# A gated recurrence and a gated linear unit: a deeper ring of squares, one x tile less, and batches of two chunks

## The chip, the core and the metric

The kernel runs on one core of a Trainium2 chip. Its engines work side by side, each through its own queue of instructions in order: TensorE (PE), VectorE (DVE), ScalarE (ACT) and GpSimd (POOL) compute, SyncE (SP) issues most of the transfers. The metric is the device time of one execution in microseconds (us); less is better.

## What is computed

The inputs are three arrays of 4 sequences, 6336 tokens and 256 features, and some small weights. In the reference's terms, cut to the core:

```python
a_t = np.exp(8.0 * sig_r * np.log(sigmoid(a_param)))      # decay, sig_r = sigmoid(r_gate)
norm = np.sqrt(np.maximum(1.0 - a_t * a_t, 1e-06))
x_gated = norm * sig_i * x                                # sig_i = sigmoid(i_gate)
h = a_t[:, t] * h + x_gated[:, t]                         # for every t: the recurrence, y[:, t] = h
gate = sigmoid(conv(y, conv_w))                           # causal, 5 taps
out = (gate * (y @ w_val)) @ w_out
```

## The kernel before

The 25344 tokens are cut into 51 tiles: 48 of 512 tokens, 3 of 256. A chunk is what one scan runs over: 23 chunks of two tiles (1024 tokens), and smaller ones at both ends (256, 512 at the front; 512, 256, 256 at the back; CHUNKS, L17). There are 28 chunks. The 256 features lie in two halves of 128 partitions, so most steps on a chunk come twice (index k = 2c + h).

A tile g or a chunk c passes through these steps, each a small function with a letter:

- load (l) and loadx (x) on SP: the gates r and i of a tile, and its x. NIN = 4 tiles of gates and NX = 5 tiles of x have buffers. store (s), also on SP, writes a tile of the output.
- tanh (t, ACT, L354): tanh of both gates at once, from which the sigmoids follow.
- u2 (u, L365 on DVE or L369 and L370 on POOL): (tanh + 1) times x, into a ring of NU = 10 tiles. The string U2 (L35) says for each tile which engine does it.
- srT (r, PE, L379): transposes of r's tanh; exp (e on ACT, L388): the decay a, into the ring aring.
- e (e on POOL, L396): a times a, into the ring ering, of NE × 512 = 4096 tokens.
- sq (q, ACT, L400): square roots, which make squares into norms in the same ring, in half the bytes. Tanh and exp lie in one table of ACT, the square root in another; ACT's table is loaded anew at each change between them. So the roots are done for several chunks at a time: UNITS (L19) says how many chunks each batch takes, and a batch is one activation, or two where its chunks are not in one piece of the ring (Shape, L92 to L103).
- nT (n, PE, L410): transposes of norms; xg (x, DVE, L417): norms times u; xT (x, PE, L426): transposes back.
- scan (s, DVE, L444): the recurrence, 1024 steps in one instruction, into yring.
- conv (c, PE, L470), tg (g, ACT, L478; tanh of the gate), val (v, PE, L486), gv (v, DVE, L496), out (o, PE, L508), and osb (o; DVE L519 or ACT L521), which copies a bank of output to SBUF for the store. The string OSB (L33) says for each of the 99 pieces of the output which engine copies it.

The order on each queue is written out by hand: ORDER (L48) holds one string of letters per engine, in which the n-th letter of a kind is the n-th job of that kind on that engine. BANK_ORDER (L61) says which of four PSUM banks each transpose or output uses. make_jobs (L130) lists the jobs with what each depends on: a tile's x load, for instance, on the input gate of tile g − NX, which frees its buffer; a square on the root and the transposes that last used its place in the ring (eold, L104). make_plan (L181) walks the strings with the costs of COST (L37) and gives all jobs in one order of start; the loop at L532 issues them. Only the strings decide the order on a queue. A queue waits where a job's inputs or its place are not there yet.

The setup ahead of the loop issues the first eight jobs of SP, makes the identity and the diagonal weights, and loads the weights wv (L292, four transfers) and wo (L296, two transfers) from POOL's queue, before POOL's first square.

Of the kernel before, what the change touches and what calls it, by code (L numbers as in the profile page):

```python
# [9 lines left out]
P = 128  # L10
# [5 lines left out]

CHUNKS = [[256], [512]] + [[512, 512]] * 23 + [[512], [256], [256]]  # L17

UNITS = [2, 1, 2, 3, 3, 3, 3, 3, 2, 2, 1, 3]  # L19
NS = 10  # L20
NE = 8
NU = 10
NY = 6
NIN = 4
NX = 5
NTR = 3
NTI = 5
NOSB = 3
# [1 line left out]
BANKS = 4  # L30
PB = dict(srT=2, nT=2, xT=2, ops=2)

OSB = "DDDDDDDDDDDAADDDDDDDDDDDDDDDDDDDDDDDDDDDDDDDDDDDDDDDDDDDDDADDDDDDDDDDAAAAADDDAAAADAAAAAADADDAAAADAA"  # L33

U2 = "DDPDDDPPDPPPPDPPPPPPPPPPPPPPDPPPPPPPPPPPPPPPPPPPPPP"  # L35

COST = dict(load=(0.05, 2.72), loadx=(0.02, 1.37), tanh=(0.11, 1.7), u2P=(0.2, 3.25), u2D=(0.2, 1.7), srT=(0.05,  # L37
            0.47), exp=(0.26, 0.86), e=(0.06, 1.83), sq=(0.2, 1.71), nT=(0.05, 0.5), xg=(0.02,
            0.58), xT=(0.05, 0.48), scan=(0.13, 2.14), conv=(0.22, 1.14), tg=(0.1, 0.83), val=(0.02,
            0.96), gv=(0.07, 1.07), out=(0.02, 0.49), osbD=(0.6, 0), osbA=(0.5, 0), store=(0.03,  # L40
            1.36))


LETTERS = dict(
    DMA=dict(l="load", x="loadx", s="store"), ACT=dict(t="tanh", e="exp", q="sq", g="tg", o="osb"),
    PE=dict(r="srT", n="nT", x="xT", c="conv", v="val", o="out"), POOL=dict(e="e", u="u2"),
    DVE=dict(u="u2", x="xg", s="scan", v="gv", o="osb"))
ORDER = dict(  # L48
    DMA=("llllxllxxxllxlxlxxxlxllxxsllxlsxxsslxlxslllsxxllssxxslslxlxxslslxsslxlxslxsllxslxsxsxlxsllxslxlslssx"
         "xlsxslxllssxsxxsllxlslsxxsxxsslsxlxslsssxxsssssssssss"),  # L50
    ACT=("teetetteeetqqttgeteetegtqegtetgetetgeettgqgetteogoetgtegtgeegtgqettegetgteegetgqgttgeetgtgetegeettgq"
         "getgettgeetgeetgtgqetgetgeettgeogqgtgetgetegtqogeoeogootgqgtteegoeogeeoeogqogoogoooggogooogogoo"),
    PE=("rrrrrrnxxnxcnxrrnrvxrcxovorcnnxorcvxnrrvncxoorrvooxcvocorovonnnnxrcxvonoxrconrvxcovxcrorxcvocvoocoov"
        "rooonnnxrxnrxnvcrnxvorcorovcxvoocxoooovnncnrnxxrcoxvorcvroxocrvrnoconvoxxocvroovnncnonrxxvcroxrncvoo"
        "rrnoxcoxvcoovcooxvronnvonorncoxrrvxcxvoorcoxonvcovnonoxcrvocxorvorncnnxxcooxrvonnvrocoxnoovxcovncovn"
        "oxrrcxvorocorrxcornvoxocvxonnvocxoovoxcnvocxooxvocoxvocoxovocvoo"),
    POOL="eeeeeeueeeeuuueueeeeeuuuuueeeeueeuuueeueeeeuuuuueueeeeeuuuueeueueeeuuueeueeuuueeueeuueeuuueeeueeeuu",
    DVE=("uuxssxsxuusxsvsvououxxsvoxsxvoosvoosovouooxxxvxssxvsxovsosvsvoooovoovooxxxosxssvxxsovoovsoovooosxoxv"
         "xxssvsoovosuxovooxvosvoosoxxvxoxssovsxoovxsoovsoovosovoxxoxoxvosvssovosvxooxoxovsovsvoxoxxsosovxxsvs"
         "vxsvoxoxovssvsxvosvxxvsvsxsovsosovsvsvov"))  # L60
BANK_ORDER = ("2220300232032030101322321213031230312121301103230301320123103021230121321321012121032312030131032110"  # L61
              "3203210321303123021032021023120103120130231030231023013203121032031230131302102302031031220131201321"
              "03120202310233203213201203302132002310232320202312303203031210")
TABLE, SEM, DMA_LAT = 1.3, 0.15, 2.2
START, ACT_START = 0.9, 4.6
FP32 = mybir.dt.float32
BF16 = mybir.dt.bfloat16
ACT = mybir.ActivationFunctionType
ALU = mybir.AluOpType


class Shape:
# [3 lines left out]
    def __init__(self, total, seq):  # L76
# [10 lines left out]
        self.apos, self.aold = self.place(NS * WIN)  # L87
        self.epos, _ = self.place(NE * WIN)
        self.ypos, self.yold = self.place(NY * WIN)


        self.runs, self.npos, batch_of = [], [], []  # L92
        for u, n in enumerate(UNITS):
            runs = []
# [35 lines left out]
def make_jobs(sh):  # L130
# [4 lines left out]
    jobs = {op: [] for ops in LETTERS.values() for op in ops.values()}  # L135
    unit_of = [u for u, n in enumerate(UNITS) for _ in range(n)]
    ends = [sum(UNITS[:u + 1]) for u in range(len(UNITS))]
    qlast = [max(q for q, (w, _) in enumerate(sh.pieces) if w == g) for g in range(len(sh.tiles))]
# [5 lines left out]
    for g, (_, n) in enumerate(sh.tiles):  # L144
        f = n / WIN
        c = sh.chunk_of[g]
        job("load", "DMA", f, [("tanh", g - NIN)])
        job("loadx", "DMA", f, [("u2", g - NX)])
        job("tanh", "ACT", f, [("load", g), ("u2", g - NTI)]
            + ([("srT", 2 * sh.chunk_of[g - NTR] + 1)] if g >= NTR else []))  # L150
        job("u2", "DVE" if U2[g] == "D" else "POOL", f, [("tanh", g), ("loadx", g)] + ([("xT", 2 * sh.chunk_of[g - NU] + 1)] if g >= NU else []), "u2" + U2[g])
        job("nT", "PE", f, [("sq", unit_of[c]), ("xg", g - PB["nT"])], None, 1)
        job("xg", "DVE", f, [("nT", g), ("u2", g)])
        job("conv", "PE", f, [("scan", 2 * c + 1), ("tg", g - 1)])
        job("tg", "ACT", f, [("conv", g), ("gv", g - 2)])
        job("val", "PE", f, [("scan", 2 * c + 1), ("gv", g - 1), ("conv", g)])
        job("gv", "DVE", f, [("tg", g), ("val", g)] + ([("out", qlast[g - 2])] if g >= 2 else []))
        job("store", "DMA", f, [("osb", q) for q, (w, _) in enumerate(sh.pieces) if w == g])
    for c, (_, n, g0, g1) in enumerate(sh.chunks):
# [3 lines left out]
        for h in range(2):  # L163
            k = 2 * c + h
            job("srT", "PE", f, [("tanh", g1 - 1), ("exp", k - PB["srT"])], None, 1)
            aold = ("scan", 2 * sh.aold[c] + h if sh.aold[c] >= 0 else -1)
            job("exp", "ACT", f, [("srT", k), aold])
            job("e", "POOL", f, [("exp", k), ("sq", eu), ("nT", sh.chunks[ed][3] - 1 if ed >= 0 else -1)])
            job("xT", "PE", f, [("xg", g1 - 1), ("scan", k - PB["xT"])], None, 1)
            job("scan", "DVE", f, [("xT", k), ("val", ylast - 1), ("conv", ylast)])  # L170
    for q, (g, i) in enumerate(sh.pieces):
        job("out", "PE", 1, [("gv", g), ("osb", q - PB["ops"])], None, 1)
        job("osb", "DVE" if OSB[q] == "D" else "ACT", 1, [("out", q), ("store", g - NOSB)], "osb" + OSB[q])
    for u, n in enumerate(UNITS):
        size = sum(sh.chunks[c][1] for c in range(ends[u] - n, ends[u])) / CHUNK
# [5 lines left out]
def make_plan(sh):  # L181
# [5 lines left out]
    for eng, letters in ORDER.items():  # L187
        todo = {op: [i for i, job in enumerate(jobs[op]) if job[0] == eng] for op in LETTERS[eng].values()}
        seq[eng] = [(op, todo[op].pop(0)) for op in (LETTERS[eng][x] for x in letters)]
        assert not any(todo.values())  # L190
    free_bank = iter(BANK_ORDER)
    for op, i in seq["PE"]:
# [5 lines left out]
    done, order, mode = {}, [], "E"  # L198
    free = dict(dict.fromkeys(seq, 0.0), DMA=START, ACT=ACT_START)
    at, left = dict.fromkeys(seq, 0), sum(len(ops) for ops in seq.values())  # L200
    while left:
        was = left
        for eng, ops in seq.items():
            while at[eng] < len(ops):
# [9 lines left out]
                free[eng] = t + dur  # L214
                done[op, i] = t + dur + (DMA_LAT if eng == "DMA" else 0.0)
                order.append((t, op, i, eng, dur))
# [8 lines left out]
def kernel(  # L225
# [11 lines left out]
    nc = tc.nc  # L237
    B, S, D = x.shape
    assert D == 2 * P, f"kernel assumes D == 256, got {D}"
    H = D // P  # L240
# [24 lines left out]
    def loadx(g):  # L265
        t0, nt = tiles[g]
        nj = nt // P
        xt = inp.tile([P, SUB, D], FP32, name="xt", tag="xt", bufs=NX)
        nc.sync.dma_start(xt[:, 0:nj, :], xf[t0:t0 + nt, :].rearrange("(p j) d -> p j d", j=nj))
        live["xt", g] = xt  # L270

    with tc.manual_schedule():
# [13 lines left out]
        b025 = const.tile([P, 1], FP32, name="b025")  # L286
        nc.vector.memset(b025[:], 0.25)
        wv = const.tile([P, H, D], BF16, name="wv")

        for hk in range(H):  # L290
            for m in range(H):
                nc.gpsimd.dma_start(wv[:, hk, m * P:(m + 1) * P].rearrange("p (h c) -> p h c", h=H),  # L292
                                    moe_w_val[hk * P:(hk + 1) * P, :].rearrange("p (h m c) -> p m h c", h=H, m=2)[:, m])
        wo = const.tile([P, H, D], BF16, name="wo")
        for h in range(H):
            nc.gpsimd.dma_start(wo[64 * h:64 * h + 64, :, :],  # L296
                                moe_w_out[h * P:(h + 1) * P, :].rearrange("(m c) n -> c m n", m=2))
        khf = const.tile([P, H], FP32, name="khf")
        wcol = const.tile([P, H, CONV_K], FP32, name="wcol")
        with tc.tile_pool(name="ps_setup", bufs=1, space=bass.MemoryType.PSUM) as ps_setup:  # L300
# [33 lines left out]

        ering = rings.tile([P, NE * WIN * H], FP32, name="ering")
        nring = ering[:].bitcast(BF16)
# [186 lines left out]
        def op_store(g, eng):  # L523
# [2 lines left out]
            nc.sync.dma_start(of[t0:t0 + nt, :].rearrange("(p j) d -> p j d", j=nj),  # L526
                              live.pop(("osb", g))[:, 0:nj, :])

        ops_by_name = dict(load=op_load, loadx=op_loadx, tanh=op_tanh, u2=op_u2, srT=op_srT, exp=op_exp, e=op_e, sq=op_sq,
                           nT=op_nT, xg=op_xg, xT=op_xT, scan=op_scan, conv=op_conv, tg=op_tg, val=op_val, gv=op_gv,  # L530
                           out=op_out, osb=op_osb, store=op_store)
        for (t, op, i, eng, dur) in plan:  # L532
            ops_by_name[op](i, eng)


# [28 lines left out]
```

## Time and profile before

| | |
|---|---|
| median of 6 runs | 315.68 us (313.38 to 317.97) |
| the profiled execution, its time | 315.39 us |
| its span, first to last instruction | 313.6 us |
| granted TensorE clock, mean | 0.964 |
| busy share: ACT, DVE, PE, POOL | 91%, 86%, 80%, 78% |
| DMA | 104.51 MB, mean 333 GB/s |

The profile is of one execution. A row of a group names the line, the engine, the operation, what it writes and reads with shapes, and how often; behind the bar come busy us and the mean duration in ns, then the idle time of the engine just before these instructions and what ended it. A wait for several things is put down to the one that came last. A busy PE is not PE at its peak, as matmuls are pipelined and their ends are modelled. The mean shares hide stages: the pipeline fills for some 45 us, runs, and drains over the last 30.

In the order of ACT's queue there are 24 table loads, 15 activations of roots in 11 groups, 51 tanhs of inputs, 56 exponentials, 51 tanhs of gates and 25 output copies.

### The profile page before, as it was taken

To read this page: it belongs to the slowest core of one execution; us is meant where nothing else is said; L and a number is where in the kernel's file an instruction comes from. 1 tells how busy PE (TensorE), PEld (TensorE's weight loads), DVE (VectorE), ACT (ScalarE), POOL (GpSimd) and SP (SyncE) were. 2 spreads that over 40 slices of the span, in tenths; PEclk is the share of its full clock that TensorE was granted. 3 is DMA by queue.
4 is the path that set the end of the run, shared out by engine and by line. 5 is a ranking of instruction groups with operands and counts; after the bars stand their busy time and mean duration, and the time that the engine had idled before them with its cause. 6 is when DMAs were issued, how large, how long until landed. Compare 5 with 4: busy or idle time off the path is not lost.

```text
span 313.6 us, 6572 instructions
## 1 busy us (share of the span) xinstructions
PE 249.9 (80%) x2561; PEld 163.2 (52%) x2591; DVE 269.5 (86%) x273; ACT 284.7 (91%) x224; POOL 245.1 (78%) x154
## 2 busy tenths in 40 slices
PE   1226765887699987996897889979899989999994
PEld 0113633554565655554654565647555755666562
DVE  4016899698999989999799899999999999998983
ACT  5799899599999999999999979999999999989553
POOL 6273599949998997899999989998997988986000
PEclk9999987799999998899899899999999999999998
DMA  7999997995999799999994999999979989843355
GB/s 234 356 397 412 409 408 293 398 344 184 366 416 414 301 301 418 420 367 375 420 413 171 324 418 414 380 382 376 416 261 366 415 298 314 324 141 144 136 203 202
DMA packets 30797, 104.51 MB, mean 333 GB/s; under 512 B 4391, under 2 KB 4654, under 8 KB 30766
## 3 DMA queue, kind: packets, MB, share of 16 engines
q1 hardware_dynamic: 29376, 103.82, 86.9%
q0 software_dynamic: 1376, 0.26, 1.0%
q8 instruction: 20, 0.33, 0.4%
q14 instruction: 11, 0.09, 0.1%
q10 hardware_dynamic: 14, 0.01, 0.0%
HBM read 78.39 MB, written 25.95 MB: 333 GB/s over the span
## 4 chain that ended last, share of the span: by engine, by line
ACT 32%; PE 23%; DVE 15%; issue 13%; POOL 9%; DMA 5%; SPq 1%; ACTq 0%; DVEq 0%; POOLq 0%
ACT tring L354 13%; PE gp L470 7%; ACT aring L388 6%; ACT ering L400 5%; POOL uring L370 5%; ACT tg L478 4%; DVE yring L444 4%; PE bank L508 4%; PE bank L410 4%; DVE osb L519 4%; POOL ering L396 3%; PE val L486 3%; DMA ri<-in_i_gate_dram 3%; DVE gv L496 3%; PE bank L426 3%
## 5 line engine op out<-in xcount | busy, mean ns | idle before, releaser
L396 POOL TENSOR_TENSOR ering<-aring 128x1024 f32<-128x1024 f32 (+2 forms) x56 | 95.5, 1721 | 35.4 <-ACT aring L388 35.4
L444 DVE TENSOR_TENSOR_SCAN yring<-aring,yring,bank 128x1024 bf16<-128x1024 f32 (+5 forms) x54 | 110.3, 2053 | 3.8 <-PE bank L426 3.7
L370 POOL TENSOR_TENSOR uring<-t,xt 128x1024 bf16<-128x1024 f32 (+1 forms) x43 | 100.8, 2345 | 4.4 <-DMA xt<-in_x_dram 0.9
L354 ACT ACTIVATE tring<-ri 128x2048 bf16<-128x2048 f32 (+1 forms) x51 | 94.3, 1865 | 1.0 <-DMA ri<-in_i_gate_dram 0.7
L470 PE MATMUL gp<-yring,diag 64*64 64x512 bf16 (+15 forms) x1196 | 68.5, 358 | 5.1 <-ACT tg L478 4.7
L388 ACT ACTIVATE aring<-bank,khf 128x1024 f32<-128x1024 bf16 (+2 forms) x56 | 61.0, 1115 | 9.7 <-PE bank L379 9.1
L508 PE MATMUL bank<-wo,gv 128*128 128x256 bf16 x396 | 58.4, 277 | 11.2 <-DVE osb L519 4.1
L496 DVE SCALAR_TENSOR_TENSOR gv<-tg,val 128x1024 bf16<-128x1024 bf16 (+1 forms) x54 | 60.5, 1124 | 6.2 <-PE val L486 4.2
L478 ACT ACTIVATE tg<-gp 128x1024 bf16<-128x1024 f32 (+1 forms) x51 | 51.3, 1005 | 8.9 <-PE gp L470 8.2
L508 PEld LDWEIGHTS <-gv 128*128 128x128 bf16 x396 | 37.2, 99 | 31.1 <-issue 16.9
L519 DVE TENSOR_SCALAR osb<-bank 128x512 f32<-128x512 f32 x74 | 48.8, 680 | 2.5 <-PE bank L508 2.1
L486 PE MATMUL val<-yring,wv 128*128 128x512 bf16 (+1 forms) x174 | 48.3, 381 | 2.9 <-DVE gv L496 0.8
L379 PE MATMUL bank<-ident_b,tring 128*128 128x128 bf16 x396 | 34.9, 235 | 17.9 <-ACT tring L354 9.0
L470 PEld LDWEIGHTS <-diag 64*64 64x64 bf16 x1196 | 31.2, 110 | 30.7 <-issue 16.0
L369 POOL TENSOR_SCALAR t<-tring 128x1024 f32<-128x1024 bf16 (+1 forms) x43 | 45.1, 1049 | 2.0
L400 ACT ACTIVATE ering<-ering,b 128x2048 bf16<-128x2048 f32 (+3 forms) x15 | 46.2, 3108 | 0.1
L410 PE MATMUL bank<-ident_f,ering 128*128 128x128 f32 x198 | 35.0, 308 | 12.5 <-ACT ering L400 8.0
L379 PEld LDWEIGHTS <-tring 128*128 128x128 bf16 x396 | 28.4, 105 | 26.5 <-ACT tring L354 13.7
L417 DVE TENSOR_TENSOR uring<-bank,uring 128x1024 bf16<-128x1024 bf16 (+1 forms) x51 | 33.3, 666 | 7.1 <-PE bank L410 7.0
L426 PE MATMUL bank<-ident_f,uring 128*128 128x128 f32 x198 | 33.3, 290 | 6.4 <-DVE uring L417 4.6
L410 PEld LDWEIGHTS bank<-ident_f,ering 128*128 128x128 f32 x198 | 28.1, 207 | 19.6 <-ACT ering L400 10.4
L365 DVE SCALAR_TENSOR_TENSOR uring<-tring,xt 128x512 bf16<-128x512 bf16 x15 | 19.8, 1362 | 15.6 <-DMA xt<-in_x_dram 15.6
(32 smaller groups left out, 104.5 us busy)
## 6 DMA issues: line engine op xcount, KB each, us to landing
ri<-in_r_gate_dram SPq DMA_DIRECT2D x48, 512.0 KB, 8.5
ri<-in_i_gate_dram SPq DMA_DIRECT2D x48, 512.0 KB, 9.1
xt<-in_x_dram SPq DMA_DIRECT2D x48, 512.0 KB, 9.0
out_dram<-osb SPq DMA_DIRECT2D x48, 512.0 KB, 5.0
ri<-in_r_gate_dram SPq DMA_DIRECT2D x3, 256.0 KB, 5.4
ri<-in_i_gate_dram SPq DMA_DIRECT2D x3, 256.0 KB, 5.3
xt<-in_x_dram SPq DMA_DIRECT2D x3, 256.0 KB, 4.2
out_dram<-osb SPq DMA_DIRECT2D x3, 256.0 KB, 2.7
```

The source lines that it names most:

```text
L354: nc.scalar.activation(out=tring[:, r:i + 1:i - r, 0:nj, :], in_=ri[:, :, 0:nj, :], func=ACT.Tanh, scale=0.5)
L370: nc.gpsimd.tensor_tensor(out=u.rearrange("p w d e -> p w e d"), in0=t1.rearrange("p (w e) d -> p w e d", e=2), in1=xt.rearrange("p (w e) ...
L379: nc.tensor.transpose(out=srT[:, col:col + P], in_=tring[:, g % NTR, j, h * P:(h + 1) * P], identity=ident_b[:])
L388: nc.scalar.activation(out=aring[:, h, a0:a0 + nt].rearrange("c (w p j) -> c w p j", p=P, j=nj), in_=live.pop(("srT", k))[:, 0:nt].rearran ...
L396: nc.gpsimd.tensor_tensor(out=ering[:, H * e0 + h * nt:H * e0 + (h + 1) * nt], in0=a, in1=a, op=ALU.mult)
L400: nc.scalar.activation(out=nring[:, 2 * H * e0:2 * H * e0 + H * m], in_=ering[:, H * e0:H * (e0 + m)], func=ACT.Sqrt, scale=-0.25, bias=b0 ...
L410: nc.tensor.transpose(out=nT[:, w * D + h * P:w * D + (h + 1) * P], in_=ering[:, n0 + w:n0 + nw * P:nw], identity=ident_f[:])
L444: nc.vector.tensor_tensor_scan(out=yring[:, h, y0 + c0:y0 + c1], data0=aring[:, h, a0 + c0:a0 + c1], data1=xT[:, c0:c1], initial=0.0 if fr ...
L470: nc.tensor.matmul(out=gp[64 * h:64 * h + 64, m, c0:c1], lhsT=diag[rows, h, kk, rows], rhs=yring[rows, h, src:src + c1 - c0], start=(sh == 0),
L478: nc.scalar.activation(out=tg[:, :, 0:nt], in_=live.pop(("gp", g))[:, :, 0:nt], func=ACT.Tanh, scale=0.5)
L496: nc.vector.scalar_tensor_tensor(out=gv[:, 0:nj, hs, :].rearrange("c j h p -> c j (h p)"), in0=tg[:, hs, 0:nt].rearrange("c h (p j) -> c j ...
L508: nc.tensor.matmul(out=ops[:, e * D:(e + 1) * D], lhsT=gv[:, 2 * i + e, hk, :], rhs=wo[:, hk, :], start=(hk == 0), stop=(hk == H - 1))
```

## The change

- NE goes from 8 to 10: the ring of squares and norms holds 5120 tokens. NX goes from 5 to 4: a tile of x in flight less.
- UNITS: 14 batches of two chunks each, where there were 12 batches of one to three.
- OSB, U2, ORDER and BANK_ORDER are new strings. OSB has 19 letters "A" (ACT) in place of 25; U2 still has eight "D" (DVE), at tiles 0 to 3, 5, 7, 8 and 20 in place of 0, 1, 3, 4, 5, 8, 13 and 28. COST has other figures for nT, xT, conv, val and out; they change only the order in which the program is built, not that on a queue.
- The weights wv and wo are loaded from POOL's queue after the second square (of chunk 0), in place of ahead of the first.

In the new order of ACT's queue there are 30 table loads and 16 activations of roots in 14 groups. The first eight jobs of SP are l l l x l l l x; they were l l l l x l l x.

```diff
-UNITS = [2, 1, 2, 3, 3, 3, 3, 3, 2, 2, 1, 3]
+UNITS = [2, 2, 2, 2, 2, 2, 2, 2, 2, 2, 2, 2, 2, 2]
-NE = 8
+NE = 10
-NX = 5
+NX = 4
-OSB = "DDDDDDDDDDDAADDDDDDDDDDDDDDDDDDDDDDDDDDDDDDDDDDDDDDDDDDDDDADDDDDDDDDDAAAAADDDAAAADAAAAAADADDAAAADAA"
+OSB = "DDDDDDDDDDDDDDDDDDDDDDDDDDDDDDDDDDDDDDDDDDDDDDDDDDDDDADDDDDDDDDDDDDDDDDDDDAAAAADDDDDAAAAAAAAAAADADA"
-U2 = "DDPDDDPPDPPPPDPPPPPPPPPPPPPPDPPPPPPPPPPPPPPPPPPPPPP"
+U2 = "DDDDPDPDDPPPPPPPPPPPDPPPPPPPPPPPPPPPPPPPPPPPPPPPPPP"
...
-    ACT=("teetetteeetqqttgeteetegtqegtetgetetgeettgqgetteogoetgtegtgeegtgqettegetgteegetgqgttgeetgtgetegeettgq"
-         "getgettgeetgeetgtgqetgetgeettgeogqgtgetgetegtqogeoeogootgqgtteegoeogeeoeogqogoogoooggogooogogoo"),
+    ACT=("teeteetqtteteetetgqteegtteettgqgetegetetgqgteegttgetegtgeqgteetgetgqgetettgeegtgqeegttgtegetgtegqegt"
+         "tgeetgtegqegttegetgoetgqegttegetgqgetegtgetgetgqeogetgootgoeoteegeqgeogeoqogogoogogooooggoo"),
...
-    POOL="eeeeeeueeeeuuueueeeeeuuuuueeeeueeuuueeueeeeuuuuueueeeeeuuuueeueueeeuuueeueeuuueeueeuueeuuueeeueeeuu",
+    POOL="eeeeeeeeueueeeuuueeeeuuuueeeueuuueeeeuueeeeuuuueeuueeuueueueeueueueueeuueueeuuueeueeuuueueeeeuueeeuu",
...
+WEIGHTS_AFTER = ("e", 1)
...
-        for hk in range(H):
-            for m in range(H):
-                nc.gpsimd.dma_start(wv[:, hk, m * P:(m + 1) * P].rearrange("p (h c) -> p h c", h=H),
...
-        for h in range(H):
-            nc.gpsimd.dma_start(wo[64 * h:64 * h + 64, :, :],
...
+        def load_weights():
+
+            for hk in range(H):
+                for m in range(H):
+                    nc.gpsimd.dma_start(wv[:, hk, m * P:(m + 1) * P].rearrange("p (h c) -> p h c", h=H),
...
+            for h in range(H):
+                nc.gpsimd.dma_start(wo[64 * h:64 * h + 64, :, :],
...
         for (t, op, i, eng, dur) in plan:
             ops_by_name[op](i, eng)
+            if (op, i) == WEIGHTS_AFTER:
+                load_weights()
```

More of the change, by code (lines that the diff above doesn't have):

```diff
@@ L31 @@
 PB = dict(srT=2, nT=2, xT=2, ops=2)
-OSB = "DDDDDDDDDDDAADDDDDDDDDDDDDDDDDDDDDDDDDDDDDDDDDDDDDDDDDDDDDADDDDDDDDDDAAAAADDDAAAADAAAAAADADDAAAADAA"
-U2 = "DDPDDDPPDPPPPDPPPPPPPPPPPPPPDPPPPPPPPPPPPPPPPPPPPPP"
+OSB = "DDDDDDDDDDDDDDDDDDDDDDDDDDDDDDDDDDDDDDDDDDDDDDDDDDDDDADDDDDDDDDDDDDDDDDDDDAAAAADDDDDAAAAAAAAAAADADA"
+U2 = "DDDDPDPDDPPPPPPPPPPPDPPPPPPPPPPPPPPPPPPPPPPPPPPPPPP"
 COST = dict(load=(0.05, 2.72), loadx=(0.02, 1.37), tanh=(0.11, 1.7), u2P=(0.2, 3.25), u2D=(0.2, 1.7), srT=(0.05,
-            0.47), exp=(0.26, 0.86), e=(0.06, 1.83), sq=(0.2, 1.71), nT=(0.05, 0.5), xg=(0.02,
-            0.58), xT=(0.05, 0.48), scan=(0.13, 2.14), conv=(0.22, 1.14), tg=(0.1, 0.83), val=(0.02,
-            0.96), gv=(0.07, 1.07), out=(0.02, 0.49), osbD=(0.6, 0), osbA=(0.5, 0), store=(0.03,
+            0.47), exp=(0.26, 0.86), e=(0.06, 1.83), sq=(0.2, 1.71), nT=(0.05, 0.53), xg=(0.02,
+            0.58), xT=(0.04, 0.46), scan=(0.13, 2.14), conv=(0.15, 1.08), tg=(0.1, 0.83), val=(0.02,
+            0.88), gv=(0.07, 1.07), out=(0.02, 0.43), osbD=(0.6, 0), osbA=(0.5, 0), store=(0.03,
             1.36))
@@ L48 @@
 ORDER = dict(
-    DMA=("llllxllxxxllxlxlxxxlxllxxsllxlsxxsslxlxslllsxxllssxxslslxlxxslslxsslxlxslxsllxslxsxsxlxsllxslxlslssx"
-         "xlsxslxllssxsxxsllxlslsxxsxxsslsxlxslsssxxsssssssssss"),
-    ACT=("teetetteeetqqttgeteetegtqegtetgetetgeettgqgetteogoetgtegtgeegtgqettegetgteegetgqgttgeetgtgetegeettgq"
-         "getgettgeetgeetgtgqetgetgeettgeogqgtgetgetegtqogeoeogootgqgtteegoeogeeoeogqogoogoooggogooogogoo"),
[L53 to L56, printed above, removed]
@@ L57 @@
-    POOL="eeeeeeueeeeuuueueeeeeuuuuueeeeueeuuueeueeeeuuuuueueeeeeuuuueeueueeeuuueeueeuuueeueeuueeuuueeeueeeuu",
[L58 to L63, printed above, removed]
+    DMA=("lllxlllxlxlxxlxlxxlllxxlxlxsxxlsxlxllssxxlslxsxsllxxlsxssllslsxxxlsllssxslxlslsxxsllxslxslsxxsxslllx"
+         "slxsxssllxlxxsxsslslxllsxsxsxllsxslxssxsxxsssssssssss"),
@@ new lines @@
+    ACT=("teeteetqtteteetetgqteegtteettgqgetegetetgqgteegttgetegtgeqgteetgetgqgetettgeegtgqeegttgtegetgtegqegt"
+         "tgeetgtegqegttegetgoetgqegttegetgqgetegtgetgetgqeogetgootgoeoteegeqgeogeoqogogoogogooooggoo"),
+    PE=("rrrrrrnxnrxrcxvxrcvrnnxnrxrnoocxxvcornrnvnocorxronvcxvooxcxronnvrocnovxncrvxroocxrocvooxvocrononcxrn"
+        "voroxconvxocvornonnrcvonxrxvorcoxocovroxvxcrvnooncooxvrocxrvocnnoorcoovxcoorvnxvonocrxvrocoxvnrocono"
+        "vxoxcrvonnocxrrxvoocnnrxcovroxovconvonnxrxcrnovcxroocvoxooovcrnnonxocxrvcrvoncovoxocovronxvrnncxnovo"
+        "cxroovxrrcorovxoocovnonrcxrovonxcxnnvxocovocxxovcoxovooxcovcovoo"),
@@ new lines @@
+    POOL="eeeeeeeeueueeeuuueeeeuuuueeeueuuueeeeuueeeeuuueeuueeuueueueeueueueueeuueueeuuueeueeuuueueeeeuueeeuu",
+    DVE=("uxsuxsussuvxuxusxsvxooussovxxvxoosxovsvoosoxxsovoxvxssoovsoovosovooxxusxvoosoxvsooxoxvxvxossovoosoov"
+         "svsxooxvoosvosoxovoxoovsoovxsoxvosvoosovxoxovossxxovossoxxvsovosovxooxvxssxovsoovoosoovxxoxsovsvxoov"
+         "oosovxsxxvsxvsvsoovoosoxxvsvxsxxvssvssvsvsovvo"))
+BANK_ORDER = ("2123321110130102331302130221230122302301230123012121132131023123012102312123210310103201301301320131"
+              "2023103130123102130231201213202310203123132010303132031321023031231202302001302313021231120312310321"
+              "20131232130321320112030212312010312032010301231210212310312231")
@@ L288 @@
         wv = const.tile([P, H, D], BF16, name="wv")
-        for hk in range(H):
-            for m in range(H):
-                nc.gpsimd.dma_start(wv[:, hk, m * P:(m + 1) * P].rearrange("p (h c) -> p h c", h=H),
-                                    moe_w_val[hk * P:(hk + 1) * P, :].rearrange("p (h m c) -> p m h c", h=H, m=2)[:, m])
         wo = const.tile([P, H, D], BF16, name="wo")
-        for h in range(H):
-            nc.gpsimd.dma_start(wo[64 * h:64 * h + 64, :, :],
-                                moe_w_out[h * P:(h + 1) * P, :].rearrange("(m c) n -> c m n", m=2))
         khf = const.tile([P, H], FP32, name="khf")
@@ L527, in op_store @@
                               live.pop(("osb", g))[:, 0:nj, :])
+        def load_weights():
+            for hk in range(H):
+                for m in range(H):
+                    nc.gpsimd.dma_start(wv[:, hk, m * P:(m + 1) * P].rearrange("p (h c) -> p h c", h=H),
+                                        moe_w_val[hk * P:(hk + 1) * P, :].rearrange("p (h m c) -> p m h c", h=H, m=2)[:, m])
+            for h in range(H):
+                nc.gpsimd.dma_start(wo[64 * h:64 * h + 64, :, :],
+                                    moe_w_out[h * P:(h + 1) * P, :].rearrange("(m c) n -> c m n", m=2))
         ops_by_name = dict(load=op_load, loadx=op_loadx, tanh=op_tanh, u2=op_u2, srT=op_srT, exp=op_exp, e=op_e, sq=op_sq,
```

## The prediction

> **What bounds the kernel now.** I read the windows first: busy time per engine in five stages that I cut at the fill, the full run and the drain. Columns: stage, its length, then busy us (instructions) of PE, PE's weight loads, DVE, ACT, POOL, then PE clock, DMA share, GB/s.
>
> ```profile
> 0.00:20.00 20.00, 4.63 (x31) 3.11 (x31) 3.97 (x18) 14.68 (x15) 9.47 (x17) 1.00 0.99 313
> 20.00:45.00 25.00, 13.69 (x111) 9.20 (x112) 17.21 (x21) 23.56 (x17) 15.67 (x10) 1.00 1.03 411
> 45.00:80.00 35.00, 26.68 (x255) 17.03 (x259) 29.90 (x27) 30.62 (x21) 29.99 (x17) 0.85 0.85 315
> 80.00:280.00 200.00, 176.25 (x1863) 116.22 (x1888) 192.08 (x182) 195.45 (x147) 182.52 (x106) 0.97 0.93 355
> 280.00:313.60 33.60, 28.66 (x310) 17.65 (x306) 26.30 (x29) 20.39 (x28) 7.41 (x8) 0.97 0.46 178
> ```
>
> ACT (ScalarE) is busy 195.45 of the 200 us in the long middle: it bounds the kernel there, with DVE (192.08) just behind. Its idle time by stage is 5.3, 1.4, 4.4, 4.6 and 13.2 us, 28.9 in all. So a change can win back at most 10.4 us of ACT idle time between 20 and 280 us; whatever it adds to ACT is added to the end, until the drain. There the bound changes: in the last stage PE is the busiest, and the timeline shows it without a gap over 0.2 us from 280 to 309.
>
> Next the waits, to see what the idle time is (engine and line, what it waited for, total us, times, longest). The first two are of the whole run, the third of 20 to 80 us, the fourth of 280 us to the end.
>
> ```profile
> POOL ering L396 <- ACT aring L388: 35.4, 21, 7.6
> DVE uring L365 <- DMA xt<-in_x_dram: 15.6, 2, 8.9
> ```
> ```profile
> ACT aring L388 <- PE bank L379: 5.7, 3, 2.4
> ```
> ```profile
> ACT tg L478 <- PE gp L470: 6.3, 5, 2.7
> ```
>
> The squares on POOL wait for the exponentials (35.4 us). No row has them waiting for a norm to be read or a batch to be rooted, which is what a full ring would look like. ACT's only sizeable wait before the drain is for transposes (5.7 us); in the drain it waits for the convolution.
>
> Last the groups with shapes apart (busy, mean ns | idle before), and ACT's timeline around a batch (start, us).
>
> ```profile
> L521 ACT ACTIVATE osb<-bank 128x512 f32<-128x512 f32 x25 | 14.7, 601 | 2.6 <-PE bank L508 2.0 <-ACT osb L521 0.6
> L400 ACT ACT_TABLE_LOAD x11 | 14.1, 1283 | 0.2
> L400 ACT ACTIVATE ering<-ering,b 128x4096 bf16<-128x4096 f32 x4 | 14.8, 3706 | 0.0
> L400 ACT ACTIVATE ering<-ering,b 128x2048 bf16<-128x2048 f32 x7 | 13.9, 1996 | 0.0
> ```
> ```profile
> 266.01 1.02 ACT L478 ACTIVATE tg<-gp 128x1024 bf16<-128x1024 f32 x1 [0.23 <-PE gp L470]
> 267.05 1.28 ACT L400 ACT_TABLE_LOAD   x1
> 268.35 2.00 ACT L400 ACTIVATE ering<-ering,b 128x2048 bf16<-128x2048 f32 x1
> 270.37 1.28 ACT L478 ACT_TABLE_LOAD   x1
> 271.66 1.02 ACT L478 ACTIVATE tg<-gp 128x1024 bf16<-128x1024 f32 x1
> 272.58 1.05 ACT L354 ACTIVATE tring<-ri 128x1024 bf16<-128x1024 f32 x1
> ```
>
> A batch of square roots costs a table load before and one after it. Neighbours without a load overlap by 0.10 us (the row at 271.66 ends at 272.68, the next starts at 272.58); around a load there is a gap of 0.02.
>
> **The change part by part.**
>
> *Batches of two (ACT, on the path).* The roots fall into 11 groups in ACT's order before, 14 after: three more groups, six more loads. Each takes 1.32 us between two instructions (267.03 to 268.35) in place of an overlap of 0.10: 1.42 us. Six are 8.5 us. The Trainium skill, page "ScalarE: Activation LUTs", section "What ACT_TABLE_LOAD costs", speaks harder against the change: about 1283 ns for the load plus about 1380 ns of drain for every switch, 2.66 us. Six would be 16.0 us. The load agrees to the ns (1283); the drain does not show: tg's row ends at 267.03, the load starts at 267.05. I take the trace, 8.5, and keep the difference of 7.5 as the upper end.
>
> *Calls.* The roots are issued as 16 activations, not 15 (a batch that wraps in the ring is cut). From 1996 ns at 2048 and 3706 at 4096, 1710 ns belong to 2048 elements, so a call's fixed part is 0.29 us: +0.3.
>
> *Output copies.* OSB has 19 "A", not 25: six leave ACT for DVE. By ACT's order 12 lay ahead of the last root, now 8; the other two leave the drain, where ACT has 13.2 us idle. The four take 0.60 less 0.10 overlap each: −2.0. On DVE the six cost 6 × 0.68 = 4.1 us. The four earlier ones (2.7) lie under DVE's 7.9 idle us between 80 and 280, the two of the drain (1.4) under its 7.3. If that cover is gone, 4.1 come on top. Eight input gates stay on DVE and 43 on POOL (U2), so both keep that sum.
>
> *Order.* 45 of the 51 tanhs of the gate (tg) precede the last root, before 44: +1.0 − 0.1 = +0.9 ahead of it.
>
> So the last root, which ends at 286.8 now (284.83 + 2.00), moves by 8.5 + 0.3 − 2.0 + 0.9 = **+7.7**.
>
> *The drain.* It takes 26.8 us from that root now, on PE. Seven tiles' tg are still open then (five full, two half), after the change six (four full, two half). The full tile that is gone cost PE 1.27 (conv) + 1.03 (val) + 1.04 (out) = 3.3 us in the drain's timeline. The last batch also shrinks from 1024 to 512 tokens, so 512 tokens' transposes of norms (0.69) and of inputs (2 × 0.44) are earlier: 1.6. Between −3.3 and −4.9, as PE has no gaps to give; I take the middle, **−4.1**.
>
> *The deeper ring and the fill.* Five chunks fit in place of four, so squares of chunk c overlay older ones. As the trace shows no wait on the ring, depth alone wins nothing visible. What it and the new orders can win is ACT's 10.4 us idle between 20 and 280. The first root now follows three tanhs and four exponentials, not five and six, and could end some 6 us earlier than 24.5; but the next takes chunks 2 and 3 together, behind eight tanhs, so chunk 2's norms come about 12 us later than now (26.4). DVE keeps busy meanwhile with input gates pulled forward (tiles 0 to 3, 5, 7, 8). Bounds: 0 and −10.4. I take half of the one sizeable row, 5.7: **−2.8**.
>
> *One x tile less (SP).* A load of x waits for the input gate four tiles back, not five; the gate loads and stores queued behind it on SP wait with it, then the tanh that needs the gates. Tiles pass at about 5.6 us (35 tanhs from the root at 77.4 to the last at 274.6) and the load takes 9.0 from issue to landing; with POOL's gate (1.07 + 2.40) that is 12.5 us, against four tiles = 22 us of cover. POOL waited 0.9 us for x in the whole run. I take 0; if the cover were gone, one tile, +5.6.
>
> *Weights behind the first squares (POOL).* The six weight DMAs (4 × 0.77 + 2 × 0.62 = 4.3 us of POOL issue) leave 1.45 to 5.7 us and follow the second square, which ended at 9.6. They end at 13.9; chunk 1's two squares (1.04 each) then end at 16.0. ACT's first root table load would run from about 15.1 to 16.4, so this is just hidden. Landing took 10.9 us (wv) and 15.0 (wo): 23.6 and 28.9 at the latest, near the new first val. PE may wait there, but the transposes for chunks 0 to 3 precede it in PE's order, so ACT has work until about 40 us. I take 0, at most +4 (the 4.3 us issue without cover). The early loads share the DMA engines with less then, at 1.0% of them: below 0.5 us. A load order that puts the first x tile fourth instead of eighth (DVE waited 8.9 us for it) serves DVE, not ACT: 0.
>
> **Sum.** The profiled execution took 315.4 us: a span of 313.6 and 1.8 around it. 315.4 + 7.7 − 4.1 − 2.8 = **316.2**. The runs' median was 315.68, so this is 0.2% above it; the profiled execution is a usual one.
>
> **The rivals.**
>
> *Faster: the idle time comes back.* The looser ring and earlier first root let ACT run without its 10.4 us, or most of it. Three quarters (7.8) and the full −4.9 in the drain give 315.4 + 7.7 − 4.9 − 7.8 = 310.4. For it: 5.8 of the 10.4 lie between 20 and 80 us, where the orders change most. Against it: between 80 and 280 only 4.6 are left, and DVE, which has only 7.9 idle there, gets 2.7 more work.
>
> *Slower: the root waits for POOL's squares.* ACT's queue is in order, so a batch's root holds everything behind it until its last square is done. In five of the new 14 batches only a tanh and a tg (2.9 us) and the load (1.28) lie between the last exponential and the root: 4.2 us of cover, for a square of 1.92 that may stand behind another or behind an input gate of 3.5. It decides where POOL finishes more than 4.2 us behind ACT; one square (1.9) late at two of the five makes 320.0, at all five 325.8, and I take three and a half: 316.2 + 6.6 = 322.8. For it: POOL is busy 182.52 of 200, and the chain of waits runs along it from 153 to 187. Against: the roots' loads waited 0.2 us in all, and three batches have the same cover now.
>
> *Slower: each switch costs the skill's drain after all*: 316.2 + 7.5 = 323.7. The rows at 266 to 272 us speak against it.
>
> *It doesn't do what it says:* the ring was no limit, no idle time returns, only ACT's sum and the drain count: 319.0.
>
> **How the numbers follow.** Likeliest, 312.5 to 318.8: 0.40. Idle time back, 308 to 312.5: 0.23. Roots wait, or nothing comes back, 318.8 to 325: 0.32. The skill's drain, x or weights uncovered: 0.05. A measurement of this kernel tells about 1% from no change (312.5 to 318.8): faster 0.23, same 0.40, slower 0.37. The range of 8 in 10 reaches into both sides, 310.4 to 322.8; the likeliest case alone spans 312.5 to 318.8.
>
> **What would show it.** Right: 30 table loads of 1283 ns with no gap; 19 output copies on ACT; the last root ending near 291.6 (286.8 + 7.7 − 2.8); a drain of 22 to 23.5 us; ACT idle between 20 and 280 near 7.6. Wrong: roots or their loads with idle time before them that POOL's squares ended (second rival); ACT idle between 20 and 280 under 4 us (first); SP's x loads waiting for POOL over the 10.0 us they do now, and tanhs waiting for DMA; PE's first val waiting for wv past 40 us.

## The result, and the profile after

The changed kernel takes 312.58 us (median of 33 runs, 310.43 to 314.44); the kernel before 314.16 us (median of 70). The ratio is 0.9967, with a 95% interval of 0.995 to 0.9984: 0.5 to 1.6 us faster, within the 1% that a single measurement can tell. Runs more than 1.5% above the fastest of the same kernel count as disturbed and are left out of the ratio and of the averages below; more of them are of the kernel before, so the ratio is nearer to 1 than the medians are, and the execution profiled ahead of the prediction (315.4 us) is one of them. Forecast were 316.2 us and a little slower; measured is a little faster.

The profiled execution after took 311.0 us, its span 309.2. Its stages, with the same columns and cuts as in the prediction:

```profile
0.00:20.00 20.00, 2.86 (x19) 1.92 (x19) 3.72 (x18) 16.08 (x16) 8.14 (x16) 1.00 0.95 339
20.00:45.00 25.00, 16.46 (x123) 10.87 (x124) 18.52 (x21) 22.23 (x16) 11.96 (x7) 0.93 0.99 359
45.00:80.00 35.00, 26.48 (x265) 18.41 (x268) 31.35 (x28) 34.91 (x24) 33.45 (x20) 0.90 1.01 386
80.00:280.00 200.00, 176.83 (x1882) 116.28 (x1908) 195.16 (x188) 196.89 (x147) 183.05 (x106) 0.98 0.94 354
280.00:309.20 29.20, 24.29 (x272) 14.74 (x273) 22.68 (x27) 19.01 (x27) 7.02 (x8) 0.97 0.37 149
```

ACT still bounds the middle. From 45 to 80 us it was busy for 30.62 us of 35 and is for 34.91 now. Its waits, of the whole run for the first two, then of 20 to 80 us, then of 280 us to the end:

```profile
POOL ering L390 <- ACT aring L382: 38.1, 17, 8.6
DVE uring L411 <- PE bank L404: 16.4, 10, 10.4
```
```profile
ACT tring L348 <- issue: 2.6, 1, 2.6
```
```profile
ACT tg L472 <- PE gp L464: 3.3, 4, 1.5
```

The wait for transposes between 20 and 80 us (5.7 us) is gone; a single one of 2.6 has come. POOL's squares wait for exponentials as before, again not for the ring. DVE sits idle for 10.4 us in the fill, before the first product with norms. The groups that answer to those of before:

```profile
L515 ACT ACTIVATE osb<-bank 128x512 f32<-128x512 f32 x19 | 11.0, 599 | 2.7 <-PE bank L502 2.3 <-ACT osb L515 0.4
L394 ACT ACT_TABLE_LOAD x14 | 18.0, 1283 | 0.2
L394 ACT ACTIVATE ering<-ering,b 128x4096 bf16<-128x4096 f32 x9 | 33.4, 3709 | 0.1
```

And ACT's timeline around the last root:

```profile
284.59 1.28 ACT L394 ACT_TABLE_LOAD   x1
285.88 1.15 ACT L394 ACTIVATE ering<-ering,b 128x1024 bf16<-128x1024 f32 x1
286.94 0.58 ACT L515 ACTIVATE osb<-bank 128x512 f32<-128x512 f32 x1
```

The last root ends at 287.0 us (285.88 + 1.15), where it ended at 286.8 before; the drain takes 22.2 us in place of 26.8. So in this pair of profiles, ACT did more work before the last root in the same time, and the whole difference of the spans is in the drain. The next table splits the span at the root, with ACT's busy and idle time from the windows. Its last two rows are later profiles of the same two programs, taken for the experiments:

| profile | busy to the last root | idle 0 to 20 | idle 20 to 80 | idle 80 to the root | drain | clock |
|---|---|---|---|---|---|---|
| before | 270.3 | 5.3 | 5.8 | 5.4 | 26.8 | 0.964 |
| after | 276.7 | 3.9 | 2.9 | 3.5 | 22.2 | 0.970 |
| before_again2 | 269.9 | 4.9 | 5.3 | 3.8 | 26.6 | 0.983 |
| after_again | 276.7 | 4.1 | 3.7 | 3.2 | 22.1 | 0.972 |

In the first pair, +6.4 − 1.4 − 3.0 − 1.8 − 4.6 make the −4.4 us between the spans (rounded). That is far more than the −1.0 of the timed runs. In the second, +6.8 − 0.9 − 1.6 − 0.6 − 4.5 make −0.8, near the timed runs. The executions of the first pair lie on opposite sides of their programs' medians (315.4 and 311.0 us), those of the second both 1 to 2 us below (312.35 and 311.55); so the second is the better one to hold against the forecast.

### The profile page after: what moved, and what is told of

It reads as the page before. It is cut to its first block, busy times and chain, and to the rows that moved or that the text cites. A ratio compares the mean times of both kernels' runs of the same rounds, so it can differ in the third digit from the quotient of the medians.

```text
span 309.2 us, 6573 instructions
## 1 busy us (share of the span) xinstructions
PE 246.9 (80%) x2559; PEld 162.2 (52%) x2591; DVE 271.4 (88%) x279; ACT 289.1 (94%) x225; POOL 243.6 (79%) x154
## 4 chain that ended last, share of the span: by engine, by line
ACT 37%; DVE 21%; PE 16%; issue 14%; DMA 7%; SPq 1%; ACTq 0%; DVEq 0%
ACT tring L348 11%; DVE yring L438 8%; ACT ering L394 7%; ACT aring L382 6%; ACT tg L472 6%; DMA ri<-in_i_gate_dram 5%; PE gp L464 5%; DVE gv L490 4%; PE bank L502 3%; DVE uring L359 3%; DVE osb L513 3%; ACT L394 3%; PE val L480 3%; PE bank L404 2%; DVE uring L411 2%
## 5 line engine op out<-in xcount | busy, mean ns | idle before, releaser
L464 PE MATMUL gp<-yring,diag 64*64 64x512 bf16 (+15 forms) x1196 | 66.9, 351 | 1.3 <-ACT tg L472 0.7
L373 PE MATMUL bank<-ident_b,tring 128*128 128x128 bf16 x396 | 36.2, 239 | 25.2 <-ACT tring L348 18.1
L513 DVE TENSOR_SCALAR osb<-bank 128x512 f32<-128x512 f32 x80 | 52.7, 682 | 1.5 <-PE bank L502 1.5
L394 ACT ACTIVATE ering<-ering,b 128x4096 bf16<-128x4096 f32 (+4 forms) x16 | 46.8, 2934 | 0.2
L373 PEld LDWEIGHTS <-tring 128*128 128x128 bf16 x396 | 29.4, 108 | 33.3 <-ACT tring L348 19.6
L464 PEld LDWEIGHTS <-diag 64*64 64x64 bf16 x1196 | 29.8, 109 | 27.5 <-issue 12.4
L420 PE MATMUL bank<-ident_f,uring 128*128 128x128 f32 x198 | 34.0, 291 | 5.8 <-DVE uring L411 2.4
L420 PEld LDWEIGHTS bank<-ident_f,uring 128*128 128x128 f32 x198 | 23.0, 146 | 16.7 <-DVE uring L411 4.7
```

The source lines that it names most:

```text
L373: nc.tensor.transpose(out=srT[:, col:col + P], in_=tring[:, g % NTR, j, h * P:(h + 1) * P], identity=ident_b[:])
L394: nc.scalar.activation(out=nring[:, 2 * H * e0:2 * H * e0 + H * m], in_=ering[:, H * e0:H * (e0 + m)], func=ACT.Sqrt, scale=-0.25, bias=b0 ...
L464: nc.tensor.matmul(out=gp[64 * h:64 * h + 64, m, c0:c1], lhsT=diag[rows, h, kk, rows], rhs=yring[rows, h, src:src + c1 - c0], start=(sh == 0),
```

## The experiments

Theory O: the new orders keep ACT fed in the fill, the shorter last batch shortens the drain, and both together just outweigh six table loads. Against it: the loads cost less than thought (slack), the weights' new place does it (W), or run-to-run variation does it (R). All ratios are to the kernel before in the same session.

### Before once more, and the place of the weights

before_again is the kernel before, unchanged. before_w_late and after_w_front move the weights alone:

```diff
 # before_w_late: the six transfers leave the setup
+            if (op, i) == ("e", 1):
+                ...
 # after_w_front: the six transfers go back into the setup
-WEIGHTS_AFTER = ("e", 1)
+WEIGHTS_AFTER = ("none", 0)
+        ...
```

> The kernel before, unchanged, for a second profile. Theory O (the new orders keep ACT fed): ACT waits again for some 5 us of transposes between 20 and 80 us, and its idle time between 20 us and the drain is again near 10 us. Theory R (run to run): the first profile of before was an unlucky execution (clock 0.85 in that stage); now the wait is below 2 us and the span nearer 311 than 313.6.

> The kernel before with the six weight transfers moved behind the first two squares on POOL, and nothing else. Theory O: no change, ratio 0.998 to 1.002, since ACT's first waits are set by its own order. Theory W (the weights' place is what helps): the first gates land earlier, ACT loses about 1.4 us less before 20 us, and the ratio is 0.996 or below.

> The changed kernel with the weights back ahead of the first square, and nothing else. Theory O: as the changed kernel, ratio to before near 0.997. Theory W: the gain goes, ratio 1.000 or above, with ACT's idle time before 20 us back at 5.3.

Measured: before_again took 316.39 us, span 314.6, with ACT idle for 6.0 us between 20 and 80 us and the same waits. Its clock was as low as in the first profile (0.963), so it leaves open that both were unlucky; before_again2, further down, settles that: at a clock of 0.983 ACT was still idle for 5.3 us there and waited 5.2 us for transposes. R falls for that stage. before_w_late: 0.998 (0.9953 to 1.0006). after_w_front: 0.9953 (0.9928 to 0.9978). With the weights back in front the gain did not go, so W is not the whole cause.

It may be part of it. ACT's idle time before 20 us was 4.9 to 5.6 us with the weights in front (before, before_again, before_again2, after_w_front) and 3.9 to 4.1 with them behind (after, after_again, before_w_late). What differs most there is the time that input tanhs wait for the transfer of their gates: 0.7, 1.1, 0.8 and 1.7 us in the first four, and 0.5 at most in the others. But some variants of the experiments below break the pattern: 4.1 and 4.6 us with the weights in front (before_6loads, before_ne10_nx4), 5.2 and 5.5 with them behind (after_ne8, after_ne8_order2). The timed runs do not decide: before_w_late's runs average 313.1 us and those of before in the same session 314.3, while the ratio's interval still takes in no change. So W may be worth up to about 1 us; this stays open.

### What a table load costs

```diff
         def op_sq(u, eng):
+            if u in (5, 6, 7):
+                nc.scalar.preload_act_table(ACT.Sqrt)
+                nc.scalar.preload_act_table(ACT.Tanh)
```

> The kernel before with two more table loads ahead of each of three batches of roots in the long middle (batches 5, 6 and 7 of 0 to 11): six loads more, no other change. My prediction's step (every load on ACT is on the path): 6 x 1.30 = 7.8 us, ratio 1.025. Rival (ACT has slack that takes them): under 4 us, ratio below 1.013. With a drain of 1.38 us for each as well: 16 us, ratio 1.05.

Measured: 1.0234 (1.0193 to 1.0275), 7.4 us for six loads, or 1.23 us each (1.0 to 1.4). ACT's busy time up to the last root rose from 269.9 (before_again2) to 277.6. So the loads are on the path, and six loads with a drain each, 16 us, lie far outside. Two limits: these six runs had a low clock (0.961 on average), and four of them, below 0.965, average 321.0 us, where those of before at such a clock take 315.8 (the table by clock stands further down); that would be 5.2 us, or 0.9 each. Part of a load may thus fall into time in which ACT would have waited. And each pair of loads stands beside a load that was there already, so this run does not test the overlap of neighbours that a new switch breaks (ACT's loads ahead of one root start at 134.51, 135.80 and 137.09 us, each 1.28 long).

### What keeps ACT waiting in the fill

In the kernel before, DVE's and ACT's timelines show the wait that ends at 56.7 us and what stands in front of it:

```profile
49.31 3.72 DVE L365 SCALAR_TENSOR_TENSOR uring<-tring,xt 128x512 bf16<-128x512 bf16 x2
52.95 1.28 DVE L417 TENSOR_TENSOR uring<-bank,uring 128x1024 bf16<-128x1024 bf16 x2
```
```profile
56.72 1.20 ACT L388 ACTIVATE aring<-bank,khf 128x1024 f32<-128x1024 bf16 x1 [2.40 <-PE bank L379]
```

An input gate of 3.7 us on DVE delays two products with norms; PE's transposes of these stand in its order ahead of the ones ACT's exponential needs. One exchange in DVE's order tests that. In the changed kernel, the tanh that waits 2.6 us needs a place that DVE's gate of tile 2 frees (the gate ends at 28.03 + 4.52 = 32.55, the tanh starts at 32.63). That gate can start earlier if the one of tile 1 goes first, into DVE's idle time:

```profile
28.03 4.52 DVE L359 SCALAR_TENSOR_TENSOR uring<-tring,xt 128x512 bf16<-128x512 bf16 x2
```
```profile
32.63 1.91 ACT L348 ACTIVATE tring<-ri 128x2048 bf16<-128x2048 f32 x1 [2.63 <-issue]
```

```diff
 # before_order, DVE
-"uuxssxsxuusxsvsvououxxsvoxs...
+"uuxssxsxuusxsvsvouoxxusvoxs...
 # after_order, DVE
-"uxsuxsussuvxux...
+"uuxsxsussuvxux...
```

> The kernel before with one change in DVE's order: the input gate that runs from 49.3 to 53.0 us goes behind the two products with norms that stand after it (letters o u x x become o x x u). Theory O (ACT idles because long input gates on DVE hold up PE's transposes, which its exponentials need): the wait of 2.4 us at 56.7 us goes, and with it 2 to 2.5 us of the time, ratio 0.993. Rival (the wait only moves on, the batch of three holds the end): 0.998 to 1.002.

> The changed kernel with one change in DVE's order: the second tile's input gate goes ahead of the first tile's product with norms (u x s u becomes u u x s). Theory O: DVE sits idle for 10.4 us there, so the later gates move up, the tanh that waits 2.6 us at 32.6 us for its place doesn't, and the ratio falls from 0.9967 to about 0.989. Rival (that idle time of ACT is not on the path): 0.996 to 0.998.

Measured: before_order 0.988 (0.9828 to 0.9933), after_order 0.9898 (0.987 to 0.9926). Part of the first goes with the granted clock, which is told of below: its five runs at 0.979 and above average 310.8 us, 2.1 less than those of before at that clock, as theory O had it. The second does not: after_order's runs had a mean clock of 0.963, those of the changed kernel 0.970. In before_order the exponential starts without a wait:

```profile
54.56 1.20 ACT L388 ACTIVATE aring<-bank,khf 128x1024 f32<-128x1024 bf16 x1
55.65 1.91 ACT L354 ACTIVATE tring<-ri 128x2048 bf16<-128x2048 f32 x1
```

ACT's idle time between 20 and 80 us fell from 5.3–6.0 to 3.6 in before_order, and from 2.9–3.7 to 1.0 in after_order. In after_order the tanh in question waits 0.55 us:

```profile
30.78 1.91 ACT L348 ACTIVATE tring<-ri 128x2048 bf16<-128x2048 f32 x1 [0.55 <-ACT aring L382]
```

So idle time of ACT in the fill is on the path, and DVE's order sets a good part of it.

### Ring and x tile, alone

```diff
 # after_ne8                 # before_ne10_nx4           # before_nx4
-NE = 10                     -NE = 8                     -NX = 5
+NE = 8                      +NE = 10                    +NX = 4
                             -NX = 5
                             +NX = 4
```

> The changed kernel with the ring back at 8 x 512 tokens, all orders kept. Theory O (depth is not what helps, no square ever waits for the ring): 0.995 to 0.999 against before, no new wait on POOL. Rival (the orders need the fifth chunk): squares wait for norms to be read, ACT's roots wait behind them, ratio above 1.005.

> The kernel before with the ring at 10 x 512 tokens and four x tiles, its own batches and orders kept. Theory O: no change, 0.998 to 1.002; x loads wait longer on SP but nothing waits for x. Rival (one x tile less costs, hidden in the changed kernel by its gains): 1.005 or more. Rival (the deeper ring alone helps): 0.997 or less.

Measured: after_ne8 0.9856 (0.9803 to 0.9909) and before_ne10_nx4 0.9889 (0.9834 to 0.9943): the deeper ring seemed to help the old orders and to harm the new ones. The first met neither of its expectations, the second the last of its rivals. With six runs each, they were repeated beside two controls.

> The kernel before once more, unchanged and timed against itself: a control for the comparisons with few runs. If they are fair, the ratio is 1.000 within its interval; if a second build of the same program can differ by 1%, the ratios of 0.986 to 0.990 seen with six runs each say little.

> The changed kernel once more, unchanged: 0.9967 as before, if runs of one build stand for the kernel; and a second profile of it. Theory O: ACT idle near 3 us between 20 and 80 us, no wait for transposes there, drain 22.2 us.

> The kernel before with the deeper ring and four x tiles, repeated, since the ratio of 0.989 came from six runs. If depth (with the orders of before) really helps: again 0.986 to 0.992, and the deeper ring is worth more than the whole change. If that was the luck of six runs: 0.997 to 1.001.

> The changed kernel with the shallower ring, repeated, since the ratio of 0.986 came from six runs. If the deeper ring costs the changed kernel time: again 0.983 to 0.989. If that was the luck of six runs: 0.994 to 0.999, as the changed kernel itself.

Measured: before_again2 1.0006 (0.998 to 1.0032) and after_again 0.9968 (0.9947 to 0.9988), as they should. before_ne10_nx4_b 0.9923 (0.9894 to 0.9952) and after_ne8_b 0.9887 (0.9858 to 0.9917): both again, somewhat smaller. Last, depth was told from the place of the buffers in memory, and from the x tile:

```diff
 # after_ne8_pad: NE = 8;  before_nx4_pad: NX = 4, NE stays 8; in both
-        ering = rings.tile([P, NE * WIN * H], FP32, name="ering")
+        ering = rings.tile([P, (NE + 2) * WIN * H], FP32, name="ering")
```

> The changed kernel with the shallower ring in use but the deeper ring's memory kept (the last 1024 tokens of it unused), so that every other buffer lies where the changed kernel has it. If depth itself cost the changed kernel its 0.7%: 0.986 to 0.990 as with the shallower ring. If it was where the buffers lie: 0.995 to 0.999 as the changed kernel.

> The kernel before with four x tiles and its ring of 8 x 512 tokens in use, in memory of 10 x 512, so that all buffers lie as in the variant with ring 10 and four x tiles. If that variant's gain (0.989 and 0.992) came from depth: now 0.998 to 1.002. If from the x tile or the place of the buffers: 0.989 to 0.993 again.

> The kernel before with four x tiles, nothing else. My prediction's step (22 us of cover, no cost): 0.998 to 1.002. If fewer x loads in flight help, because the gates' loads share the DMA engines with less: 0.988 to 0.993.

Measured: after_ne8_pad 0.9898 (0.9843 to 0.9953), as with the shallow ring. before_nx4_pad 1.0001 (0.9963 to 1.0039) and before_nx4 1.0005 (0.998 to 1.003): the x tile and the place of the other buffers do nothing visible, NE does. Part of what it does goes with the granted clock, which differs from run to run of one program. These are averages over the sessions that have the clock on record:

| clock of the run | before: us (runs) | changed kernel: us (runs) |
|---|---|---|
| below 0.965 | 315.8 (20) | 313.0 (9) |
| 0.965 to 0.972 | 315.0 (28) | 312.6 (26) |
| 0.972 to 0.979 | 314.0 (73) | 312.2 (7) |
| 0.979 and above | 312.9 (19) | 311.4 (6) |

All twelve runs of the deep ring with the old orders lay above 0.972, and ten above 0.979. These ten average 311.3, against 312.9 of before; with the new orders, fourteen runs of the shallow ring at 0.979 and above average 310.3, against 311.4 for the six of the changed kernel. So some half of each effect goes with the clock. A single trace says little on this. The row of the granted clock over 40 slices, in before, in before_ne10_nx4, and in before_again2, the same program as the first:

```profile
PEclk9999987799999998899899899999999999999998
```
```profile
PEclk9999987799999999999999999999999999999998
```
```profile
PEclk9999989799999999999899999999999999999999
```

The dips to 0.8 between 118 and 180 us are missing in the second, but all except one are missing in the third too: they belong to one execution and do not show what the ring does; only the counts of runs do. Why depth goes with the clock, and what the rest is, stays open; no trace shows a wait on the ring. One rival was not separated: NE also decides which batches wrap in the ring. With the new batches, after_ne8 needs 20 activations of roots where the changed kernel needs 16; ACT works 0.6 us longer for it (277.3 against 276.7), but a first half that ends earlier may serve the engines behind it. With the old batches it is 15 either way, cut at other places. Five x tiles beside the deeper ring were not tried.

### Both edits of DVE's order, with the shallow ring

In the changed kernel ACT's longest wait after 80 us (2.44 us) stands behind a gate of 5.0 us on DVE, from 109.4 to 114.5 us. Here that gate goes behind the scan after it:

```profile
117.82 1.20 ACT L382 ACTIVATE aring<-bank,khf 128x1024 f32<-128x1024 bf16 x1 [2.44 <-PE bank L373]
```

```diff
-NE = 10
+NE = 8
 # DVE
-"uxsuxsussuvxux...ovooxxusxvoosox...
+"uuxsxsussuvxux...ovooxxsuxvoosox...
```

> The changed kernel with the shallower ring and two edits of DVE's order (the second input gate earlier, as tried; and the gate of tile 20, 5.0 us long on DVE, behind the scan after it). If ACT's waits of 2.6 and 2.4 us are on the path and add to the ring's effect: 0.976 to 0.982, the fastest of all. If they do not add: 0.986 to 0.990.

Measured: 0.9915 (0.9887 to 0.9942), no better than either alone. The wait is gone in its trace, but its runs' mean clock was 0.962, where the shallow ring's runs had 0.980 to 0.983. So the edits do not add in the time; whether they would at an equal clock is not shown. The lowest medians remain those of the changed kernel with NE = 8: 309.90, 310.10 and, with the memory kept, 311.00 us.

## Why the prediction was wrong, by its own steps

**Where the sum failed.** The terms of the forecast, against the two pairs of profiles of the unaltered programs (us):

| term | forecast | before, after | before_again2, after_again |
|---|---|---|---|
| ACT's work ahead of the last root | +7.7 | +6.4 | +6.8 |
| the drain | −4.1 | −4.6 | −4.5 |
| ACT's idle time from 20 us to the last root | −2.8 | −4.8 | −2.2 |
| ACT's idle time before 20 us | 0 | −1.4 | −0.9 |
| sum | +0.8 | −4.4 | −0.8 |

Large terms nearly cancel, so errors of 1 us turn the sign. The steps that failed are two: the work of the added switches was over-sized by about 1 us, and the idle time before 20 us was put at nothing. The first is the surer one: in the profiles before, before_again and before_again2, and after and after_again, ACT's work and the drain agree within 0.6 us for each program, but the idle times differ by up to 2.8 between executions.

**ACT's work ahead of the last root: +7.7 in the sum, +6.8 measured.** The counts were right: 30 loads, 19 copies, 16 activations of roots, and each load takes 1283 ns. What failed is the price of 1.42 us for a load, with 0.10 for an overlap of neighbours lost at each (and 0.10 again for each copy that is gone). That loss did not come. Up to the last root, the durations of ACT's instructions add up to 286.2 us in before_again2 and 293.0 in after_again; its busy time is 269.9 and 276.7, so neighbours overlap by 16.3 us in both (16.0 in both of the first pair). There are 8 fewer pairs of neighbours without a load between them, 149 for 157, but only 11 of them are now parted by a wait, where it was 19. An instruction that no longer waits overlaps its neighbour again, and the sum had left that out.

**The idle time before 20 us: nothing in the sum, −0.9 measured.** The prediction looked for gains between 20 and 280 us alone and put the earlier gate loads below 0.5 us. How much of this is the weights' new place and how much luck of the execution is open (see W above). The last root, forecast to end 4.9 us later, ended 3.7 later (283.9 and 287.6).

**The drain: −4.1, measured −4.5.** Right in its mechanism. It takes 22.1 or 22.2 us in all profiles with the new orders and 26.5 to 26.8 with the old. The upper end of the two bounds (4.9) was nearer than the middle: PE had no gaps to give, as the prediction itself said.

**Idle time after 20 us: −2.8, measured −2.2.** Between 20 and 80 us the old orders gave 5.0 to 6.3 us in all profiles but before_order's, the new ones 2.9 to 3.7 in all but after_order's, so it does come back there. Half of a row was a choice, and that it came near was luck. The reason given for the fill was wrong in one point: DVE was not kept busy by gates pulled forward, but idle for 10.4 us. And the 10.4 us of ACT's idle time were those of one execution at a low clock: between 20 and 280 us the kernel before has 10.4 and 11.0 us at 0.964 and 0.963, but 9.0 at 0.983.

**The base.** The prediction called its execution, 315.4 us, "a usual one". The median of 70 runs is 314.16, so 1.2 of the 3.6 us between 316.2 and 312.6 is the base. This part does not touch the sign. The clock does touch the size: in the table by clock above, the change gains 1.5 us at 0.979 and above and 2.8 below 0.965, while the changed kernel's runs have a lower clock on average (0.970 against 0.974), which takes some of the gain back.

**Other costs taken at nothing.** The x tile: 1.0005, right; SP's x loads wait 30.0 us in the trace (13.8 + 16.2) in place of 12.0, and nothing waits for them. The weights as a cost: the first root's load started at 13.9 and the root at 15.2 without a gap over 0.1 us between them, and no val waited for wv. "Depth alone wins nothing visible" holds for waits, not for time: NE alone moved both kernels by about 1%, in opposite directions.

**The rivals.** Roots waiting for squares: the loads ahead of them waited 0.2 us in all, as before. The skill's drain: six loads at 2.66 would be 16.0 us; measured are 7.4, so here the measurement stands against the Trainium skill's "ScalarE: Activation LUTs", section "What ACT_TABLE_LOAD costs", for the drain, and with it for the 1283 ns. Idle time all coming back: 6.0 to 6.4 us between 20 and 280 us are still there in the three profiles after, after_again and after_w_front, where the first rival needed under 4.

## What to carry to other kernels

Where a change adds work to the bounding engine and removes some at the end, the sign hangs on small differences of large terms: measure the price of the added instruction alone (six more of them, one experiment) before trusting a sum, and count overlaps that waits had broken as well as those that the new instruction breaks. Take the profiled execution's place among the runs, and its clock, before using its idle time as something to win back. In queues held in order, look for a long instruction of one engine ahead of a short one that a third engine needs; moving one letter was worth more here than the whole change.

## What was not expected of the hardware

An input gate on DVE takes some 0.65 us per half when POOL is idle, and up to 2.5 (averaged over the two halves) when POOL runs. In the changed kernel's timeline, DVE's rows of two halves (start, us):

```profile
43.31 1.31 DVE L359 SCALAR_TENSOR_TENSOR uring<-tring,xt 128x512 bf16<-128x512 bf16 x2
109.42 5.04 DVE L359 SCALAR_TENSOR_TENSOR uring<-tring,xt 128x512 bf16<-128x512 bf16 x2
```

and POOL's at these times, with nothing between 35.9 and 44.4:

```profile
44.44 1.94 POOL L390 TENSOR_TENSOR ering<-aring 128x1024 f32<-128x1024 f32 x1 [8.55 <-ACT aring L382]
...
109.21 2.38 POOL L364 TENSOR_TENSOR uring<-t,xt 128x1024 bf16<-128x1024 f32 x1
111.53 6.54 POOL L390 TENSOR_TENSOR ering<-aring 128x1024 f32<-128x1024 f32 x3
```

POOL's own three squares take 6.54 us there, where three by themselves are 5.6 to 5.8. This fits what the Trainium skill, page "SBUF — State Buffer", section "SBUF: two separate sides", says of a port pair shared by GpSimd and a DVE instruction with two inputs in SBUF: whichever starts first holds it for its whole instruction, and the other waits. No run here tests the ports apart. The planner's single cost for this gate cannot see it, and long gates of this kind stood ahead of the waits that the order edits took away.

The granted clock goes with a larger difference in time than this change makes: 312.9 us at 0.979 and above, 315.8 below 0.965, for one and the same program. That the clock is the cause is not shown.
